# Paired 96-row loads, loads queued behind the moves, and no landing gate: a linear-attention and gated feed-forward kernel

## The chip, the cores and the metric

The kernel runs on one core of one Trainium2 chip. The metric is device time in microseconds (us); lower is better. The core has five engines that run side by side and wait for each other by semaphores: PE (matrix multiply), DVE (vector), ACT (scalar activation), POOL (GpSimd) and SP (SyncE, which here only issues DMA transfers). Each engine works through its own instructions in order, so an instruction that waits holds up everything behind it on that engine.

## The reference

A recurrent attention (a decaying state for each head) feeds a gated feed-forward block with a three-tap convolution. Cut to what matters:

```python
# batch 4, heads 8, sequence 768, head size 48; d_ff 1024
for t in range(S):
    cur = einsum('bhd,bhe->bhde', u * k[t], v[t])
    y[t] = einsum('bhd,bhde->bhe', r[t], state + cur)
    state = w * state + einsum('bhd,bhe->bhde', k[t], v[t])
x = y.transpose(0, 2, 1, 3).reshape(B, S, 384)
h = maximum(x @ w_in, 0)                        # 384 -> 1024
conv_out = sum over k of conv_w[k] * h shifted by k - 1
out = (h * sigmoid(conv_out)) @ w_out           # 1024 -> 384
```

## The kernel before

**Tiling.** The sequence is cut into 24 groups of 128 tokens (6 to a batch), each of two chunks of 64. The 8 heads are 4 pairs; in each pair x=0 is the even head and x=1 the odd one. For a group the core loads `KR` (k and r with the head dimension on partitions: even heads on rows 0 to 47, odd heads on rows 64 to 111, 4 KB to a row), and `TOK` (k, r and v with tokens on partitions). In HBM a group's `krd` block has 112 rows: odd heads in rows 0 to 47, 16 filler rows, even heads in rows 64 to 111. There are four buffers of each tile (NBUF). A group is brought in by five transfers in `load(g)`: two of 48 rows for `KR` (192 KB each), one of 128 rows for k and r of `TOK` (384 KB), two of 64 rows for v (96 KB each).

**Stages.** `prep(g)` multiplies `KR` by powers of the decay (DVE, one instruction of 112x1024, called KR below) and works on `TOK` (three products, mostly on POOL, a reduction QQ on DVE, and the diagonal SC). `visit(g, av, su)` is one run of small matmuls on PE: for group g the outputs AV, and for group g+1 the scores SP and the state update UP. Visit numbers below count from 1: visit 1 holds only the scores and update of group 0; visit n holds the outputs of group n-2 and the scores of group n-1. Behind it ACT (XH) and DVE (XL) split the outputs into two parts in `XT`, and six DMA moves of 16 rows each (L628) put the fourth head pair's rows in place. For the first NSEL=3 groups PE does this itself, by an extra pass over that pair (`av3`, copies `Y7`, selection matmuls `SEL`), and there are no moves.

`first(i)` (f1) is a tile of the first feed-forward product: 9 matmuls into one of three PSUM buffers HP, then on ACT a rectifier, one tap (CV) and a sigmoid (SG), on DVE two more taps (L656) and the gate (L660), then the gated tile split for `second` (f2), the second product. There are 8 units of some 384 tokens with 8 f1 tiles each; unit 0 needs the outputs of groups 0 to 2, unit 1 those of groups 2 to 5. The weights come in 8 pieces of w_in and 6 of w_out (`convert`: ACT, DVE TENSOR_SCALAR and SCALAR_TENSOR_TENSOR, then a cast and a remainder) through three staging buffers ST.

**What sets the order.** All instructions are first recorded with estimated durations; `Plan.order` simulates the engines with these numbers and puts out one fixed order for each engine. A transfer is entered with its share x of transfer time, scaled by XFER. `gate(i)` is the landing gate: a load or weight transfer (class ld or wd) may not start before the transfers sent ahead of it, but for the last AHEAD=2.5 of x, have landed; L746 turns this into a real wait on the chip. The moves (class mv) are not gated. Where PE has nothing to do for a while the plan lets it run small fill matmuls (L740) with no use for the result.

Apart from the gate, the transfers use eight completion counters in turn (DMAHW0 to 7 in the rows below), and a transfer waits for the one that had its counter before it, eight transfers earlier.

```python
for x in (1, 0):        # L385, in load(g)
    dma([], [...], KR[i][64 * x:64 * x + D], krd[g, 64 - 64 * x:112 - 64 * x], 0.45, 0.63, "ldK")
...
PE.matmul(UP[rows[x], n:n + D], TOK[j][xs[x], 0, p, c], TOK[j][xs[x], 2, p, c], start=True, stop=True)   # L572
...
visit(g, True, g + 1 < NG)      # L711
if g + NBUF < NG:
    load(g + NBUF)              # L713: no read named, so the plan is free to put it ahead of the moves
```

## Time and profile before

| | us |
|---|---|
| three runs | 311.65, 308.57, 311.37 |
| their median | 311.37 |
| the profiled execution, from outside | 310.83 |
| its span, first to last instruction | 309.1 |
| its mean granted PE clock | 0.989 of full speed |

The profile is one execution. Its times are counted from the start of the span; 310.83 - 309.1 = 1.73 us lie around it. "Busy" of PE counts its fill matmuls too. A row of the timeline gives start, length, engine, line, operation, tiles and count, and in brackets the idle time of the engine ahead of it and what ended that. A transfer's row on SP is its issue; it lands some microseconds later. In the waits view the row "SPq ... <- DMA" is time in which the issuing queue stood still until some transfer had landed.

### The profile page before, as it was taken

Reading aid. Unit: us, or ns where it says so; the run is one execution under the profiler, and the core shown is the slowest. Engines: PE = TensorE matmul, PEld = TensorE weight load, DVE = VectorE, ACT = ScalarE, POOL = GpSimd, SP = SyncE. Lnnn points to the kernel's source line nnn. Section 1 sums busy time; section 2 is a strip of 40 time slices with the busy share of each in tenths; the row PEclk is TensorE's granted clock in tenths of the full one; section 3 lists DMA queues with packets and bytes.
Section 4 is the critical chain, followed back from the end, with each engine's and each line's share of the span. In section 5 each row is a group of like instructions: output and inputs, shape, how many; then the busy total and the mean of one; then the engine's idle time right before and its main releaser. Section 6 shows DMA issues by size and latency. Waiting matters only on the chain.

```text
span 309.1 us, 10281 instructions
## 1 busy us (share of the span) xinstructions
PE 282.5 (91%) x4272; PEld 262.0 (85%) x4272; DVE 222.8 (72%) x400; ACT 178.0 (58%) x395; POOL 170.8 (55%) x202
## 2 busy tenths in 40 slices
...
GB/s 178 214 212 216 222 225 130 182 184 210 204 156 104 213 179 130 120 119 90 123 76 154 94 114 131 160 104 106 125 56 38 30 14 39 38 27 27 0 51 51
DMA packets 24654, 37.46 MB, mean 121 GB/s; under 512 B 4832, under 2 KB 18208, under 8 KB 24608
## 3 DMA queue, kind: packets, MB, share of 16 engines
...
q8 instruction: 33, 0.54, 0.8%
q10 hardware_dynamic: 304, 0.59, 0.6%
q14 instruction: 13, 0.11, 0.1%
HBM read 30.01 MB, written 4.72 MB: 112 GB/s over the span
## 4 chain that ended last, share of the span: by engine, by line
PE 51%; DMA 20%; DVE 11%; POOL 6%; ACT 6%; issue 3%; SPq 2%; DVEq 0%; ACTq 0%; POOLq 0%
PE HP L647 19%; PE PO L680 19%; DMA TOK<-in_krt_dram 7%; DMA KR<-in_krd_dram 6%; DVE CV L656 4%; PE SP L562 4%; PE HP L680 3%; DMA ST<-in_w_in_dram 3%; PE AV L575 2%; POOL TOK L358 2%; POOL GG L358 2%; PE AV L568 2%; DMA XT<-XT 2%; PE UP L572 2%; DVE SG L660 2%
## 5 line engine op out<-in xcount | busy, mean ns | idle before, releaser
L647 PE MATMUL HP<-XT,wi 128*128 128x384 f32 (+1 forms) x576 | 115.0, 344 | 13.0 <-DVE SG L660 5.3
L647 PEld LDWEIGHTS HP<-XT,wi 128*128 128x128 f32 x576 | 103.0, 191 | 16.6 <-DVE SG L660 6.6
L680 PE MATMUL PO<-GG,wo 128*128 128x382 f32 (+1 forms) x528 | 106.1, 343 | 2.9 <-issue 1.4
L680 PEld LDWEIGHTS PO<-GG,wo 128*128 128x128 f32 x528 | 92.0, 189 | 6.2 <-ACT OS L686 2.7
L358 POOL TENSOR_TENSOR GG<-SG,GG 128x386 fp32r<-128x386 f32 (+1 forms) x46 | 46.8, 1018 | 82.8 <-ACT GG L662 82.8
L656 DVE SCALAR_TENSOR_TENSOR CV<-HP,cw,CV 128x382 f32<-128x382 f32 (+1 forms) x128 | 78.0, 614 | 19.3 <-ACT CV L653 17.8
L659 ACT ACTIVATE SG<-CV 128x382 f32<-128x382 f32 (+1 forms) x64 | 33.5, 524 | 44.2 <-DVE CV L656 43.6
L660 DVE TENSOR_TENSOR SG<-HP,SG 128x382 f32<-128x382 f32 (+1 forms) x64 | 35.5, 554 | 20.8 <-ACT SG L659 20.5
L575 PE MATMUL AV<-SC,TOK 64*48 64x64 f32 x768 | 46.4, 218 | 0.8 <-DVE SC L589 0.8
L562 PE MATMUL SP<-KR 48*64 48x64 f32 x768 | 46.0, 230 | 0.1
L568 PE MATMUL AV<-KR,SS 48*48 48x64 f32 x704 | 43.2, 219 | 3.1 <-DVE XT L358 3.1
L662 ACT CAST GG<-SG 128x382 fp32r<-128x382 f32 (+1 forms) x64 | 32.7, 511 | 20.4 <-DVE SG L660 19.8
L562 PEld LDWEIGHTS SP<-KR 48*64 48x64 f32 x768 | 38.1, 134 | 6.2 <-issue 4.2
L572 PE MATMUL UP<-TOK 64*48 64x48 f32 x704 | 40.5, 206 | 0.4 <-DVE SS L358 0.4
L652 ACT ACTIVATE HP<-HP 128x384 f32<-128x384 f32 (+1 forms) x64 | 30.4, 476 | 15.6 <-PE HP L647 15.3
L358 DVE TENSOR_TENSOR KR<-KR,TKR 112x1024 f32<-112x1024 f32 (+1 forms) x26 | 29.3, 1132 | 12.8 <-DMA KR<-in_krd_dram 12.5
L653 ACT ACTIVATE CV<-HP,cw 128x382 f32<-128x382 f32 (+1 forms) x64 | 37.1, 580 | 1.0
L575 PEld LDWEIGHTS AV<-SC,TOK 64*48 64x48 f32 x768 | 35.2, 120 | 1.1 <-DVE SC L589 1.1
L568 PEld LDWEIGHTS AV<-KR,SS 48*48 48x48 f32 x704 | 32.0, 120 | 4.1 <-DVE XT L358 3.8
L572 PEld LDWEIGHTS UP<-TOK 64*48 64x48 f32 x704 | 33.0, 123 | 0.6 <-DVE SS L358 0.6
L358 POOL TENSOR_TENSOR TOK<-TOK,TH 128x384 f32<-128x384 f32 x24 | 24.7, 1028 | 10.5 <-DVE TOK L358 9.4
L508 POOL TENSOR_TENSOR SC<-eye,QQ 128x512 f32<-128x512 f32 x23 | 24.1, 1046 | 6.9 <-PE AV L575 3.1
...
## 6 DMA issues: line engine op xcount, KB each, us to landing
...
XT<-XT SPq DMA_DIRECT2D x126, 16.0 KB, 1.9
```

The source lines that it names most:

```text
L358: op(eng, d, rd, wr, lambda e: e.tensor_tensor(**kw), cls, port=not psum)
L562: PE.matmul(SP_[xs[x], p, c], KK[j][rows[x], p, t], RR[j][rows[x], p, t], start=True, stop=True)
L568: PE.matmul(outs[x], state(2 * g + c)[rows[x], p], RR[i][rows[x], p, t], start=not sel, stop=False)
L572: PE.matmul(UP[rows[x], n:n + D], TOK[j][xs[x], 0, p, c], TOK[j][xs[x], 2, p, c], start=True, stop=True)
L575: PE.matmul(outs[x], TOK[i][xs[x], 2, p, c], SC[g % 2][xs[x], p, c], start=first and c == 0 and not sel, stop=True)
L647: PE.matmul(hp, wi[a][:, j, fs], X[:, x, j, t], start=(j == 0 and k == 0), stop=(j == 2 and k == 2))
L653: op("act", act(n, 0.155), [H_, "cw"], [("T", ti)], lambda e: A.activation(t1, hp[:, 1:n + 1], AF.Copy, scale=cw[:, 3 * f + 1:3 * f + 2]), ...
L656: op("dve", dve(n) + 0.06, [H_, "cw"], [("T", ti)], lambda e, k=k: V.scalar_tensor_tensor(out=t1, in0=hp[:, k:n + k], scalar=cw[:, 3 * f + ...
L659: op("act", act(n, 0.097), [("T", ti)], [("SG", ti)], lambda e: A.activation(sg, t1, AF.Sigmoid))
L660: op("dve", dve(n), [H_], [("SG", ti)], lambda e: V.tensor_tensor(out=sg, in0=hp[:, 1:n + 1], in1=sg, op=ALU.mult), "GG")
L662: op("act", act(n), [("SG", ti)], [("GH", gi)], lambda e: A.copy(gh, sg))
L680: PE.matmul(po[:, :n], wo[a][:, f, ms], g2[x], start=(f == 0 and j == 0), stop=(f == NF - 1 and j == 2))
```

## The change

- **One transfer for two groups' halves.** Rows 64 to 111 of group g's block (even heads) and rows 0 to 47 of the next one's (odd heads) lie next to each other in HBM. `load_kr(g)` brings these 96 rows in one transfer into rows 16 to 111 of the `KR` tile (g+1) mod 4. A tile thus holds the even heads of g and the odd heads of g+1. A transfer of 48 rows (odd heads of group 0) goes ahead of them, and the last one has 48 rows. So 25 `KR` transfers stand in place of 48, and 25 decay products in place of 24; the first two tiles are done in halves. The load sent after visit g's part is `load_kr(g+3)`, where `KR` of g+4 went before; `TOK` stays at g+4.
- **Rows 0 to 15** of `KR` are zero (Z=16). The x=0 matmuls contract 64 rows instead of 48, and the x=0 weights of UP have 64 columns instead of 48 (`TOK` has 16 more words ahead of its data).
- **Loads behind the moves.** `moved(g)` makes a load "read" the last move of group g, so the plan puts it behind that move on SP.
- **No landing gate.** AHEAD=100 is never reached, so L746's waits go. The eight completion counters stay.
- **NSEL=2.** Group 2 loses its selection pass and gets six moves.
- Estimates: XFER 1.3 to 1.1, and other x for nearly every transfer. A clearing of UP goes, four of 128x16 in `TOK` come, the `KR` clearings have other rows.

```diff
-NSEL = 3
-AHEAD = 2.5
+NSEL = 2
+AHEAD = 100.0
+XK = 1.1
+HR = slice(0, 64), slice(64, 112)
+DR = slice(Z, 64), slice(64, 112)
-SWITCH, XFER = 0.13, 1.3
+SWITCH, XFER = 0.13, 1.1
...
+        rows_ = krd.rearrange("g q a p t -> (g q) a p t")
+        def moved(g):
+            return [("Xm", g // GPB % 2, g % GPB, 64, 2)] if g >= NSEL and AFTER else []
+        def load_kr(g, rd=()):
+            i = (g + 1) % NKR
+            a, b = 112 * g + 64, 112 * g + 64 + 2 * D
+            lo, hi = DR[0].start, DR[1].stop
...
+            dma(rd, ks, KR[i][lo:hi], rows_[a:b], 0.45, XK, "ldK")
-        def load(g, eng="sp"):
+        def load(g, eng="sp", rd=()):
             i = g % NBUF
-            for x in (1, 0):
-                dma([], [(n, i, x) for n in ("KK", "RR")], KR[i][64 * x:64 * x + D], krd[g, 64 - 64 * x:112 - 64 * x], 0.45, 0.63, "ldK")
-            dma([], [("tK", i), ("tR", i)], TOK[i][:, 0:2], krt[g], 0.55, 1.05, "ldT", eng)
+            dma(rd, [("tK", i), ("tR", i)], TOK[i][:, 0:2], krt[g], 0.55, 0.98, "ldT", eng)
...
-        op("dve", 0.7, [], ["SUu"], lambda e: V.memset(UP, 0.0))
...
-                        rows = [slice(64 * x, 64 * x + D) for x in range(2)]
+                        rows = HR
-                                PE.matmul(SP_[xs[x], p, c], KK[j][rows[x], p, t], RR[j][rows[x], p, t], start=True, stop=True)
+                                PE.matmul(SP_[xs[x], p, c], KK[tj[x]][rows[x], p, t], RR[tj[x]][rows[x], p, t], start=True, stop=True)
-                                PE.matmul(UP[rows[x], n:n + D], TOK[j][xs[x], 0, p, c], TOK[j][xs[x], 2, p, c], start=True, stop=True)
+                                PE.matmul(UP[rows[x], n:n + D], TOKP[j][xs[x], Z * x + (2 * p + c) * D:Z + (2 * p + c + 1) * D], TOK[j][xs[x], 2, p, c], start=True, stop=True)
...
+                if g + NKR - 1 < NG:
+                    load_kr(g + NKR - 1, moved(g))
                 if g + NBUF < NG:
-                    load(g + NBUF)
+                    load(g + NBUF, rd=moved(g))
```

The first place is SP where the tiles are loaded for the second time. ST is a staging buffer of weights, the number behind a tile's name is its buffer, the last number can be passed over; a wait DMAHWn is one for a transfer to land. Before (from the fifth group's k and r on):

```order
L362 DMA TOK0_65<-in_krt_dram 128x768 [waits DMAHW7_49,DVE_49,PE_49]
L362 DMA KR0_61<-in_krd_dram 48x1024 [waits DMAHW4_49,DMAHW1_49,PE_49]
L362 DMA KR0_61<-in_krd_dram 48x1024 [waits DMAHW2_49]
L362 DMA TOK0_65<-in_vt_dram 64x384 [waits DMAHW6_49,PE_49]
L362 DMA TOK0_65<-in_vt_dram 64x384 [waits DMAHW3_49,PE_49]
L362 DMA TOK1_66<-in_krt_dram 128x768 [waits DMAHW0_49,DVE_49,PE_49]
L362 DMA KR1_62<-in_krd_dram 48x1024 [waits DMAHW4_49,PE_49]
L362 DMA KR1_62<-in_krd_dram 48x1024 [waits DMAHW5_49]
L362 DMA ST0_103<-in_w_in_dram 128x768 [waits DMAHW7_49,DVE_49,Pool_49]
```

And now, from the same transfer up to the first move:

```order
L369 DMA TOK0_65<-in_krt_dram 128x768 [waits DVE_49,DMAHW6_49,PE_49,Pool_49]
L369 DMA ST2_105<-in_w_in_dram 128x768 [waits DMAHW7_49]
L369 DMA KR0_61<-in_krd_dram 96x1024 [waits DMAHW0_49,PE_49]
L369 DMA TOK0_65<-in_vt_dram 64x384 [waits DMAHW1_49,PE_49]
L369 DMA TOK0_65<-in_vt_dram 64x384 [waits DMAHW2_49,PE_49]
L369 DMA TOK1_66<-in_krt_dram 128x768 [waits DMAHW3_49,DVE_49,PE_49]
L369 DMA ST0_103<-in_w_in_dram 128x768 [waits DMAHW4_49,Pool_49]
L369 DMA KR1_62<-in_krd_dram 96x1024 [waits DMAHW5_49,PE_49]
L369 DMA TOK1_66<-in_vt_dram 64x384 [waits DMAHW6_49,PE_49]
L369 DMA TOK1_66<-in_vt_dram 64x384 [waits DMAHW7_49,PE_49]
L369 DMA ST1_104<-in_w_in_dram 128x768 [waits DMAHW0_49,Pool_49]
L369 DMA XT0_79<-XT0_79 16x2x128 [waits DMAHW1_49,DVE_49]
```

The counters now simply come round in turn (6, 7, 0, 1 ...), where before other landings stood among them; the fifth weight piece (the reload of ST1, which waits for POOL) stands ahead of group 2's moves.

The second place is DVE ahead of the first f1 tile's taps, the first row on a CV tile. PO is the buffer of a weight piece in conversion, and one TENSOR_SCALAR and one SCALAR_TENSOR_TENSOR on ST make up one piece. Before:

```order
L589 COPY_PREDICATED SC1_70<-mask_110,SP_120 128x512
L358 TENSOR_TENSOR XT0_79<-AV_122,XT0_79 128x3x128
L358 TENSOR_TENSOR SS0_71<-MM1_76,UP_121 112x192
L358 TENSOR_TENSOR KR1_62<-KR1_62,TKR_123 112x1024
L528 TENSOR_REDUCE QQ0_77<-TOK0_65 128x8
L475 TENSOR_SCALAR PO_127<-PO_127 128x384
L477 SCALAR_TENSOR_TENSOR ST0_103<-ST0_103,PO_127 128x384
L656 SCALAR_TENSOR_TENSOR CV0_83<-HP0_124,cw_119,CV0_83 128x382 x2
```

And now:

```order
L507 SCALAR_TENSOR_TENSOR ST1_104<-ST1_104,PO_127 128x384
L365 TENSOR_TENSOR wi1_116<-ST1_104,wi0_115 128x3x128
L562 TENSOR_REDUCE QQ1_78<-TOK1_66 128x8
L365 TENSOR_TENSOR SS1_72<-MM0_75,UP_121 112x192
L624 COPY_PREDICATED SC0_69<-mask_110,SP_120 128x512
L365 TENSOR_TENSOR XT0_79<-AV_122,XT0_79 112x4x128
L365 TENSOR_TENSOR SS2_73<-MM1_76,UP_121 112x192
L505 TENSOR_SCALAR PO_127<-PO_127 128x384
L507 SCALAR_TENSOR_TENSOR ST2_105<-ST2_105,PO_127 128x384
L691 SCALAR_TENSOR_TENSOR CV0_83<-HP0_124,cw_119,CV0_83 128x382
```

Before, the piece shown is the fourth; now it is the sixth, and visit 5 and the split of group 3's outputs also stand ahead of the first tap. On PE, visit 5 and 18 fill matmuls ahead of it now come before the first f1 tile, where before visit 4 was followed by 8 fills and two f1 tiles. From visit 8 on PE's order of visits, f1 and f2 is the same as before.

More of the change, by code (lines that the diff above doesn't have):

```diff
@@ L28 @@
 NBUF = 4
+NKR = 4
+AFTER = 1
+Z = 16
 NT = 3
@@ L310, in sb @@
             return [cst.tile(shape, dt, name=f"{name}{i}") for i in range(n)]
-        KR = sb([112, 2, NP, GT], F32, "KR", NBUF)
+        KR = sb([112, 2, NP, GT], F32, "KR", NKR)
         KK, RR = [x[:, 0] for x in KR], [x[:, 1] for x in KR]
-        TOK = sb([128, 3, NP, 2, D], F32, "TOK", NBUF)
+        TOKP = sb([128, Z + 3 * NP * 2 * D], F32, "TOK", NBUF)
+        TOK = [x[:, Z:].rearrange("q (a p c d) -> q a p c d", a=3, p=NP, c=2) for x in TOKP]
         SC = sb([128, NP, 2, C], F32, "SC", 2)
@@ L378, in krz @@
         def krz(i):
-            op("pool" if i else "dve", 1.0, [], [n for n in kr(i) if n[2] == 0], lambda e: e.memset(KR[i][32:64], 0.0), "KRz")
+            n = 64 if i == 0 else Z
+            op("pool" if i > 1 else "dve", 1.0, [], [n for n in kr(i) if n[2] == 0], lambda e: e.memset(KR[i][0:n], 0.0), "KRz")
         krz(0)
-        def load(g, eng="sp"):
+        krz(1)
+        for i in range(NBUF):
+            op("pool", 0.06, [], [("tK", i)], lambda e, i=i: G.memset(TOKP[i][:, 0:Z], 0.0), "KRz")
@@ new lines, in rwkv_ffn_kernel @@
+        rows_ = krd.rearrange("g q a p t -> (g q) a p t")
[5 more added lines that the diff above has]
+            lo, hi = DR[0].start, DR[1].stop
+            if g < 0:
+                a, lo = 0, 64
+                b = D
+            if g == NG - 1:
+                b, hi = a + D, 64
+            ks = [k for k in kr(i) if (k[2] == 0 or hi > 64) and (k[2] == 1 or lo < 64)]
+            dma(rd, ks, KR[i][lo:hi], rows_[a:b], 0.45, XK, "ldK")
@@ L392, in rwkv_ffn_kernel @@
+        load_kr(-1)
+        load_kr(0)
         load(0, "act")
-        dma([], ["uu"], uu, ut, 0.55, 0.4, "ldU")
+        dma([], ["uu"], uu, ut, 0.55, 0.25, "ldU")
         op("pool", 0.1, [], ["mask"], lambda e: G.memset(mask, 1))
         op("pool", 0.1, [], ["ident"], lambda e: G.memset(ident, 1.0))
+        for o, n, b in ((0, 64, Z), (64, 48, 0)):
+            op("pool", 0.2, [], ["ident"], lambda e, o=o, n=n, b=b: G.affine_select(
+                out=ident[o:o + n], in_=ident[o:o + n], pattern=[[1, D]],
+                compare_op=ALU.is_equal, fill=0.0, base=b, channel_multiplier=-1))
@@ L407, in rwkv_ffn_kernel @@
                 compare_op=ALU.is_equal, fill=0.0, base=0, channel_multiplier=-1))
-        for i in range(1, NBUF):
+        for i in range(2, NKR):
             krz(i)
```

39 lines of the change are left out of this document (21 added, 18 removed).

## The prediction, made before the changed kernel was run

> **What bounds the kernel now.** I read the page's busy line first, then PE's rows with idle time ahead of them, then the chain of work that ended last, then SP's queue.
>
> The page's first part, then PE's busy time by stage (columns: stage, its length, busy time of PE, weight loads, DVE, ACT, POOL, PE's granted clock, share and rate of the DMA engines):
>
> ```profile
> PE 282.5 (91%) x4272; PEld 262.0 (85%) x4272; DVE 222.8 (72%) x400; ACT 178.0 (58%) x395; POOL 170.8 (55%) x202
> ```
> ```profile
> 34.14:66.72 32.58, 26.24 (x463) 22.93 (x463) 28.06 (x53) 24.42 (x57) 27.44 (x29) 0.95 0.64 184
> 66.72:136.87 70.15, 64.40 (x1019) 60.25 (x1019) 57.90 (x100) 44.17 (x97) 55.17 (x59) 1.00 0.60 161
> 136.87:309.10 172.23, 165.17 (x2192) 159.54 (x2192) 112.81 (x200) 98.06 (x209) 62.04 (x69) 1.00 0.27 76
> ```
>
> The stages are cut where units begin: the first f1 tile starts at 34.14, unit 1's at 66.72. PE is the bound from 136.87 on (7.1 us idle in 172). Ahead of that it is fed too slowly: 6.3 us idle in the second stage, where DVE is busy 86%, and 5.8 in the third. PE's large gaps:
>
> ```profile
> 34.14 2.10 PE L647 MATMUL HP<-XT,wi 128*128 128x384 f32 x8 [1.47 <-ACT XT L618]
> 57.08 3.28 PE L647 MATMUL HP<-XT,wi 128*128 128x384 f32 x10 [2.52 <-DVE SG L660]
> 66.72 1.85 PE L647 MATMUL HP<-XT,wi 128*128 128x388 f32 x9 [0.85 <-DMA XT<-XT]
> 87.34 1.87 PE L647 MATMUL HP<-XT,wi 128*128 128x388 f32 x9 [0.78 <-DVE SG L660]
> 136.87 1.46 PE L647 MATMUL HP<-XT,wi 128*128 128x388 f32 x6 [2.17 <-DVE QQ L528]
> 171.21 1.82 PE L647 MATMUL HP<-XT,wi 128*128 128x384 f32 x9 [2.17 <-DMA XT<-XT]
> ```
>
> The chain shows why the feed is slow: loads one behind another, each sent only when an earlier one has landed.
>
> ```profile
> 23.05 5.60 DMA TOK<-in_krt_dram
> ...
> 29.29 5.71 DMA TOK<-in_krt_dram
> ...
> 35.06 4.07 DMA ST<-in_w_in_dram
> ...
> 39.19 5.36 DMA TOK<-in_krt_dram
> ...
> 44.61 1.02 POOL TOK L358
> ```
>
> The buffer of the load at 39.19 came free with visit 4 (28.71 to 31.6, below). It is sent 7.6 us later, behind the landings above, and POOL starts on it at 44.61. SP's waits say the same: on k and r of TOK alone the queue stood 24.8 us for landings.
>
> ```profile
> SPq L362 <- DMA TOK<-in_krt_dram: 24.8, 15, 3.6
> ```
>
> **The change part by part.** *Transfer.* At 143.91 both 48-row halves of KR run alone, then at 151.69 the 128 rows of TOK, with KR behind them (SP's issues, then the DMA rate, the last column):
>
> ```profile
> 143.91 0.79 SPq L362 DMA_DIRECT2D KR<-in_krd_dram  x2
> ...
> 151.69 0.53 SPq L362 DMA_DIRECT2D TOK<-in_krt_dram  x1
> 152.35 0.81 SPq L362 DMA_DIRECT2D KR<-in_krd_dram  x2
> ```
> ```profile
> 144.75:145.50 0.75, 0.75 (x6) 0.75 (x5) 0.75 (x2) 0.73 (x4) 0.75 (x1) 1.00 0.81 202
> 153.50:154.75 1.25, 1.25 (x8) 1.25 (x8) 1.25 (x3) 0.53 (x1) 0.73 (x2) 1.00 1.00 357
> 154.75:155.75 1.00, 1.00 (x7) 1.00 (x7) 0.88 (x3) 0.08 (x1) 0.51 (x1) 1.00 0.97 223
> ```
>
> So 48 rows move at 202 to 223 GB/s with the engines nearly full, 128 rows at 357. The pair's 393 KB take 1.76 to 1.95 us; at TOK's rate 1.10. The 96 rows are nearer to 128 than to 48, so I take 0.7 us less of DMA time a group (0 to 0.85). It counts only where a landing ends a wait, that is through the terms below; one issue fewer saves SP some 0.4 us (0.79/2).
>
> The Trainium skill, "SBUF — State Buffer", section "Door 1: The DMA port swizzle", says that rows 0 to 63 reach only eight of SBUF's sixteen DMA ports and rows 64 to 127 the other eight. By its 218 and 436 GB/s the pair would take an estimated 1.80 us and the joint transfer 0.90, so 0.9 saved where my rows give 0.7. The trace agrees in kind, 202 to 223 against 357, and the measured rates decide.
>
> *Start of the first f1 tile.* Group 2 trades its selection pass for six moves. The rows that price it:
>
> ```profile
> 26.25 0.32 PE L568 MATMUL AV<-KR,SS 48*48 48x64 f32 x4 [2.13 <-DVE XT L358]
> 28.71 0.37 PE L562 MATMUL SP<-KR 48*64 48x64 f32 x2
> 31.62 1.05 PE L740 MATMUL HP<-wz 128*128 128x256 bf16 x8
> ```
> ```profile
> L624 ACT CAST XT<-AV 112x512 fp32r<-112x512 f32 x21 | 12.3, 586 | 4.1 <-PE AV L575 3.1 <-PE UP L572 1.0
> L358 DVE TENSOR_TENSOR XT<-AV,XT 112x512 fp32r<-112x512 f32 x21 | 14.2, 679 | 0.0
> L362 SPq DMA_DIRECT2D XT<-XT x126: 585/592/1632, 45.9 to 264.8; - x126
> DMA to landing us min/median/max: 1.8/1.9/6.3
> ```
> ```profile
> 30.20 1.03 POOL L358 TENSOR_TENSOR wi<-ST,wi 128x384 fp32r<-128x384 f32 x1
> 8.65 1.28 DVE L358 TENSOR_TENSOR KR<-KR,TKR 112x512 f32<-112x512 f32 x2 [0.31 <-ACT TKR L440]
> ```
>
> Without av3 and its copies visit 4 can stand where av3 stood, 26.25 (it waited for the split of group 1). It lasts 2.9 us (28.71 to 31.62), so 29.15; XH 0.59 and XL 0.68: 30.4; six issues at 0.592: 34.0; landing 1.9: 35.9. Late bound: the moves stand on SP behind the fifth weight piece, whose buffer POOL gives free when the second piece's remainder is done, 31.2 in the row: 31.2 + 3.55 + 1.9 = 36.7. The extra product of the first tile (half products of two tiles, 1.28 us more on DVE ahead of visit 1) could push all that to 38.0. I take 36.5: later than before's 34.14 by 2.4, but with visit 5 already done.
>
> *Unit 0, 34.14 to 66.72.* DVE works 28.06 us of 32.58.
>
> ```profile
> L475 DVE TENSOR_SCALAR PO<-PO 128x384 int32<-128x384 int32 (+2 forms) x11 | 6.1, 552 | 2.7 <-ACT PO L472 2.7
> L477 DVE SCALAR_TENSOR_TENSOR ST<-ST,PO 128x384 int32<-128x384 int32 (+1 forms) x10 | 5.7, 575 | 0.1
> L589 DVE COPY_PREDICATED SC<-mask,SP 128x512 f32<-128x512 int32 x24 | 17.7, 739 | 0.6 <-PE UP L572 0.5
> L358 DVE TENSOR_TENSOR SS<-MM,UP 112x192 f32<-112x192 f32 x40 | 13.7, 343 | 0.9 <-POOL MM L605 0.9
> ```
> ```profile
> 36.25 1.22 DVE L358 TENSOR_TENSOR KR<-KR,TKR 112x1024 f32<-112x1024 f32 x1 [1.31 <-DMA KR<-in_krd_dram]
> 55.87 0.70 DVE L475 TENSOR_SCALAR PO<-PO 128x512 int32<-128x512 int32 x1 [1.25 <-ACT PO L472]
> ```
>
> Two to three more weight pieces are now converted ahead of f1 (2.5 x 1.13 = 2.8 us), and visit 5's mask and two state sums (0.74 + 0.69 = 1.4). Left: 28.06 - 2.8 - 1.4 = 23.9. Of the 4.5 us idle, 1.31 and 1.25 follow from late landings (ACT's PO waits for a weight load); I let half of these go, so 3.2 stay. Unit 1 then begins at 36.5 + 23.9 + 3.2 = 63.6, 3.1 us earlier than 66.72. Bounds: 38.0 + 23.9 + 4.5 = 66.4 (0.3 gained), and 35.9 with all landing waits gone (2.0 idle): 61.8, 4.9 earlier.
>
> *Units 1 and 2.* The gaps at 87.34 and 136.87 are DVE standing in order at a KR product whose load has not landed:
>
> ```profile
> 85.59 1.22 DVE L358 TENSOR_TENSOR KR<-KR,TKR 112x1024 f32<-112x1024 f32 x1 [2.39 <-DMA KR<-in_krd_dram]
> ```
>
> I take half of 0.78 + 2.17, so 1.5 (0 to 2.95). *Later.* At 171.21 the unit waits for its last moves. Six issues and a landing stay, TOK and v still stand ahead, only KR's two issues leave: 0.4 of 2.17 (0 to 0.8). On the other side 176 weight loads of UP get 64 columns instead of 48. Weight loads of 48 and 64 columns take 123 and 134 ns here:
>
> ```profile
> L572 PEld LDWEIGHTS UP<-TOK 64*48 64x48 f32 x704 | 33.0, 123 | 0.6 <-DVE SS L358 0.6
> L562 PEld LDWEIGHTS SP<-KR 48*64 48x64 f32 x768 | 38.1, 134 | 6.2 <-issue 4.2 <-DVE CV L656 0.5 <-DVE SC L589 0.4
> ```
>
> With two records each, 352 x 11 ns = 3.9 us if all showed, 0 if matmuls cover them. The x=1 load of 48 columns runs beside, so I take 0.5. Contracting 64 rows instead of 48 changes no count of columns; I price it at 0 inside that bound. Clearings and the lost clearing of UP lie before DVE's first product at 8.65, where the decay powers set the time: 0.
>
> *Sum.* 309.1 - 3.1 - 1.5 - 0.4 + 0.5 = 304.6 for the span; with the 1.73 around it 306.3 for such an execution. The median of the runs is 0.54 above the profiled one (311.37 against 310.83), so **306.9**.
>
> **Rivals.** *A, more goes:* f1 at 35.9, all waits for landings gone: 309.1 - 4.9 - 2.95 - 0.8 + 2.27 = 302.7 (2.27 = 1.73 + 0.54). For it: the chain above is nearly all landings. Against: DVE and POOL are busy over 78% up to 136.87.
>
> *B, hidden or not done:* the gate goes, but every transfer still waits for the one eight places earlier, and KR's lead is a visit shorter. f1 at 38.0, DVE's waits unchanged: unit 1 at 66.4, nothing gained later, 0.5 lost on UP: 309.1 - 0.3 + 0.5 + 2.27 = 311.6. For it: SP also waits for ACT and PE, which the change leaves. Against: the 7.6 us at 39.19.
>
> *C, slower by moves behind loads.* Up to eight transfers may be under way and the gate no longer keeps the queue short, so a unit's last moves land late, PE waiting as at 66.72 and 171.21. Landings reach 6.3 us in the row above, where 1.9 is the median. If the seven later units each start 1.5 us later: 306.9 + 10.5 = 317.4. From 0.64 us a unit (4.5/7) the gain is used up. Against it: the loads are now put behind the moves of the same group.
>
> The Trainium skill bears on C: "DMA: Bandwidth & Descriptors", section "Queues, rings and completion order", has each DMA engine take its descriptors in the order of the ring, so that a move would queue behind every load sent before it.
>
> **How the numbers follow.** Forecast 0.50, A 0.16, B 0.22, C 0.12. A measurement of this kernel tells about 1% (3.1 us) from no change, so faster is below 308.3, slower above 314.5. Faster: A and nearly all of the forecast's cases, 0.62; same: B and the forecast's rest, 0.27; slower: C's larger part, 0.11. The range 301.5 to 313 takes in A and B and leaves out C and a little of A.
>
> **What would show it.** Right: the first f1 later, near 36.5, with visit 5 ahead of it; unit 1's first tile near 63.6; KR's DMA rate near 350 GB/s; SP's wait for TOK landings well under 24.8; no KR wait over 2 us on DVE near 136. Wrong: unit 1 no earlier than 66, moves landing in over 3 us at unit starts (C), or visits longer by 0.1 us and more (UP's weights).

## The result, and the profile after

The changed kernel takes 311.93 us (median of 20 runs, 309.13 to 313.48), the kernel before 310.16 us in the same series (20 runs, 304.64 to 315.16). The ratio of after to before is 1.013, with a 95% interval of 1.0085 to 1.0174: a little slower, where 306.9 us and faster was forecast, and inside the band that the prediction called no change (308.3 to 314.5). Each ratio in this document leaves out a kernel's runs over 1.5% above its fastest (here 14 of the 20 of before, none of after), so it makes after look slower than the two medians over all runs do, which lie 0.6% apart (1.8 us). The profiled execution of after has a span of 311.7 us (313.4 from outside), that of before 309.1.

The page's first part for after, and PE's busy time by stage, cut where it was for before and with the stretch ahead (the columns are the same):

```profile
PE 283.1 (91%) x4249; PEld 264.1 (85%) x4249; DVE 229.0 (73%) x411; ACT 177.1 (57%) x401; POOL 160.4 (51%) x194
```
```profile
10.43:34.14 23.71, 18.19 (x532) 15.57 (x532) 14.02 (x27) 9.59 (x29) 21.42 (x24) 0.93 0.85 237
34.14:66.72 32.58, 23.88 (x443) 21.52 (x444) 26.18 (x50) 22.12 (x54) 21.50 (x24) 0.90 0.55 161
66.72:136.87 70.15, 67.04 (x1038) 63.44 (x1037) 61.10 (x106) 46.48 (x107) 49.50 (x53) 1.00 0.51 148
136.87:311.70 174.83, 165.97 (x2191) 159.45 (x2189) 119.89 (x212) 95.95 (x207) 61.83 (x68) 1.00 0.27 82
```

PE is busy as long as before (283.1 us against 282.5). Between 34.14 and 66.72 it is idle 8.7 us, where it was 6.3, and DVE, which had the most to do there, is less busy than before (26.2 against 28.1), so it waits more. The DMA engines are busier ahead of that (237 GB/s from 10.43 to 34.14, before 216) and less busy in it (161 against 184). In the next stretch PE is idle 3.1 us instead of 5.8, a gain; in the last 8.9 instead of 7.1. PE's rows with idle time, and the starts of unit 0 (40.17) and unit 1 (69.11):

```profile
35.92 0.27 PE L597 MATMUL SP<-KR 64*64 64x64 f32 x2 [2.25 <-DVE SC L624]
40.17 2.00 PE L682 MATMUL HP<-XT,wi 128*128 128x384 f32 x10 [0.30 <-DMA XT<-XT]
48.03 0.27 PE L597 MATMUL SP<-KR 64*64 64x64 f32 x2 [2.87 <-DVE KR L365]
58.22 0.33 PE L597 MATMUL SP<-KR 64*64 64x64 f32 x4 [2.00 <-DVE KR L365]
69.11 1.84 PE L682 MATMUL HP<-XT,wi 128*128 128x388 f32 x9
```

The large gaps of before (57.08, 136.87, 171.21) are gone. New ones stand ahead of visits 6 and 7, both for DVE's product on KR.

PE's granted clock also halves here in three stretches of 3.4 us (from 12.2, 36.1 and 60.0; in before in two, from 26.7 and 57.4), and the matmuls in them take longer: the three of f1 in the last stretch take 522 to 686 ns, where the median of all is 338 (the clock is the third column from the end; the second row gives ns, least, median and most):

```profile
60.01:63.42 3.41, 3.08 (x77) 2.88 (x68) 3.41 (x8) 3.37 (x8) 3.17 (x4) 0.50 0.11 24
```
```profile
L682 PE MATMUL HP<-XT,wi x576: 331/338/686, 40.2 to 293.6; 128*128 128x384 f32 x96, 128*128 128x388 f32 x96
```

Each stretch begins within 2 us of a gap of PE (ahead of 12.06, 35.92 and 58.22), but the longest gap, ahead of 48.03, has none behind it. What sets the clock no run tests.

The waits of all engines (what waited, for what: total us, times, longest):

```profile
POOL TOK L365 <- DMA TOK<-in_krt_dram: 25.7, 13, 3.7
DVE KR L365 <- DMA KR<-in_krd_dram: 15.1, 15, 2.6
PE PO L715 <- ACT OS L721: 6.9, 9, 1.2
```
```profile
SPq L369 <- DMA TOK<-in_krt_dram: 8.0, 6, 3.5
```

SP waits 8.0 us for TOK landings where it waited 24.8. But DVE now waits for KR 15 times, 15.1 us in all (before: 8 times, 12.5 us), and PE waits at PO for the output copy OS nine times (before: twice, 1.4 us). POOL's wait for TOK grows most, from 4.5 us; but it is still 15.5 us in e10 below, the fastest of all runs. The waits for KR and at PO belong together, as one place late in the span shows (start, length, engine, line, operation; in brackets the idle time ahead and what ended it):

```profile
188.74 1.22 DVE L365 TENSOR_TENSOR KR<-KR,TKR 112x1024 f32<-112x1024 f32 x1 [1.52 <-DMA KR<-in_krd_dram]
...
191.37 0.60 DVE L691 SCALAR_TENSOR_TENSOR CV<-HP,cw,CV 128x382 f32<-128x382 f32 x1
192.05 0.52 ACT L694 ACTIVATE SG<-CV 128x382 f32<-128x382 f32 x1 [4.69 <-DVE CV L691]
...
192.89 0.47 ACT L721 ACTIVATE OS<-PO 128x386 f32<-128x386 f32 x1
...
193.42 1.32 PE L715 MATMUL PO<-GG,wo 128*128 128x386 f32 x6 [1.21 <-ACT OS L721]
```

DVE stands 1.52 us at a product whose load has not landed. The taps CV stand behind that on DVE, the sigmoid SG waits for them on ACT, the copy OS, which frees PO, stands behind SG on ACT, and PE waits for PO. Read from the bottom the row names ACT; the one that is late is a DMA several steps away.

Why it is late: SP's issues of moves and KR loads, and DVE's products:

```profile
35.00 4.86 SPq L369 DMA_DIRECT2D XT<-XT  x6
...
41.05 0.38 SPq L369 DMA_DIRECT2D KR<-in_krd_dram  x1
...
43.84 5.07 SPq L369 DMA_DIRECT2D XT<-XT  x5
...
50.28 0.58 SPq L369 DMA_DIRECT2D XT<-XT  x1
50.96 0.52 SPq L369 DMA_DIRECT2D KR<-in_krd_dram  x1
```
```profile
46.76 1.22 DVE L365 TENSOR_TENSOR KR<-KR,TKR 112x1024 f32<-112x1024 f32 x1 [1.18 <-DMA KR<-in_krd_dram]
...
56.94 1.22 DVE L365 TENSOR_TENSOR KR<-KR,TKR 112x1024 f32<-112x1024 f32 x1 [2.62 <-DMA KR<-in_krd_dram]
```

The load behind the product of 46.76, which visit 6 needs, is sent at 41.05; in the kernel before the one for visit 6 went out at 29.91. A joint tile holds the even heads of one group and the odd heads of the next, so it serves one visit more than a tile of one group did. With four buffers its successor can go out one visit later. It also stands behind the moves now (those of group 2 end their issue at 39.86, those of group 3 at 50.86). Which of the two counts, and what the lost gate does, the trace alone can't say.

### The profile page after: what moved, and what is told of

Read it like the earlier page. It is cut to its first block, busy times and chain, and to the rows that moved or that the text cites. A ratio compares the mean times of both kernels' runs of the same rounds, so it can differ in the third digit from the quotient of the medians.

```text
span 311.7 us, 10202 instructions
## 1 busy us (share of the span) xinstructions
PE 283.1 (91%) x4249; PEld 264.1 (85%) x4249; DVE 229.0 (73%) x411; ACT 177.1 (57%) x401; POOL 160.4 (51%) x194
## 4 chain that ended last, share of the span: by engine, by line
PE 33%; DMA 21%; DVE 21%; POOL 8%; ACT 7%; SPq 5%; issue 4%; ACTq 0%; POOLq 0%
PE PO L715 15%; DMA KR<-in_krd_dram 13%; PE HP L682 12%; DMA TOK<-in_krt_dram 6%; DVE CV L691 6%; SPq L369 5%; POOL TOK L365 5%; DVE KR L365 4%; PE HP L715 3%; DVE SG L695 3%; DMA ST<-in_w_in_dram 2%; ACT SG L694 2%; DVE SC L624 2%; DVE XT L365 2%; DVE GG L365 2%
## 5 line engine op out<-in xcount | busy, mean ns | idle before, releaser
L682 PE MATMUL HP<-XT,wi 128*128 128x384 f32 (+1 forms) x576 | 112.8, 341 | 2.5 <-DVE SG L695 2.1
L365 POOL TENSOR_TENSOR GG<-SG,GG 128x382 fp32r<-128x382 f32 (+1 forms) x37 | 37.6, 1017 | 70.4 <-ACT GG L697 70.2
L597 PE MATMUL SP<-KR 48*64 48x64 f32 (+1 forms) x768 | 50.1, 237 | 9.4 <-DVE KR L365 6.1
L597 PEld LDWEIGHTS SP<-KR 48*64 48x64 f32 (+1 forms) x768 | 44.4, 141 | 15.3 <-DVE KR L365 5.5
L607 PE MATMUL UP<-TOK 64*48 64x48 f32 (+1 forms) x704 | 45.7, 217 | 1.5 <-POOL TOK L365 1.2
L603 PE MATMUL AV<-KR,SS 64*48 64x64 f32 x704 | 44.6, 223 | 2.4 <-DVE XT L365 2.2
L607 PEld LDWEIGHTS UP<-TOK 64*48 64x48 f32 (+1 forms) x704 | 41.7, 136 | 2.0 <-POOL TOK L365 1.3
L365 DVE TENSOR_TENSOR KR<-KR,TKR 112x1024 f32<-112x1024 f32 (+1 forms) x27 | 30.6, 1139 | 15.5 <-DMA KR<-in_krd_dram 15.1
L610 PEld LDWEIGHTS AV<-SC,TOK 64*48 64x48 f32 x768 | 38.2, 124 | 0.2 <-DVE SC L624 0.2
L603 PEld LDWEIGHTS AV<-KR,SS 64*48 64x48 f32 x704 | 34.6, 124 | 3.2 <-DVE XT L365 2.9
L365 POOL TENSOR_TENSOR TOK<-TOK 128x384 f32<-128x384 f32 x23 | 23.3, 1011 | 25.8 <-DMA TOK<-in_krt_dram 25.7
```

The lines of the kernel that those rows point to most:

```text
L365: op(eng, d, rd, wr, lambda e: e.tensor_tensor(**kw), cls, port=not psum)
L597: PE.matmul(SP_[xs[x], p, c], KK[tj[x]][rows[x], p, t], RR[tj[x]][rows[x], p, t], start=True, stop=True)
L603: PE.matmul(outs[x], state(2 * g + c)[rows[x], p], RR[ti[x]][rows[x], p, t], start=not sel, stop=False)
L607: PE.matmul(UP[rows[x], n:n + D], TOKP[j][xs[x], Z * x + (2 * p + c) * D:Z + (2 * p + c + 1) * D], TOK[j][xs[x], 2, p, c], start=True, sto ...
L610: PE.matmul(outs[x], TOK[i][xs[x], 2, p, c], SC[g % 2][xs[x], p, c], start=first and c == 0 and not sel, stop=True)
L682: PE.matmul(hp, wi[a][:, j, fs], X[:, x, j, t], start=(j == 0 and k == 0), stop=(j == 2 and k == 2))
```

## The experiments

Times are medians; "against before" is the difference to the median of the kernel before in the same series (310.2 to 312.3 us). Where it and the ratio point apart (e2, e15), neither is read as a change against before. KR is DVE's wait for KR loads, PO is PE's wait at PO for OS, clock is PE's mean granted clock, all three of the profiled execution (before: 12.5, 1.4, 0.989). For e7 and e13 that execution took 321.6 and 315.9 us, more than their medians, for e8 305.9 us, 5 us less than its median.

The plan makes a new order for each edit, so no run changes one thing alone: with the gate off (e6), for example, ACT has 411 instructions where it had 395. And the runs made from the kernel before keep the old estimates (XFER and x), those made from the changed kernel have the new ones; no run changes the estimates by themselves.

| run | us | against before | ratio (95%) | KR | PO | clock |
|---|---|---|---|---|---|---|
| the changed kernel | 311.9 | +1.8 | 1.013 (1.009 to 1.017) | 15.1 | 6.9 | 0.984 |
| e1_before_wide | 310.4 | -1.6 | 1.000 (0.995 to 1.005) | 11.5 | 1.4 | 0.989 |
| e2_no_tie | 310.9 | -1.1 | 1.008 (1.003 to 1.013) | 12.0 | 3.8 | 0.988 |
| e3_three_sel | 315.9 | +3.9 | 1.011 (1.005 to 1.018) | 10.7 | 3.0 | 0.978 |
| e4_gate | 317.6 | +5.6 | 1.021 (1.016 to 1.026) | 16.0 | 7.0 | 0.973 |
| e5_before_short_lead | 319.1 | +6.8 | 1.028 (1.022 to 1.035) | 22.6 | 6.0 | 0.973 |
| e6_before_no_gate | 305.7 | -6.6 | 0.988 (0.980 to 0.996) | 1.1 | 0.3 | 0.977 |
| e7_fewer_gg | 320.1 | +7.8 | 1.027 (1.018 to 1.036) | 27.1 | 5.5 | 0.973 |
| e8_five_kr | 311.3 | -1.1 | none given | 10.4 | 5.0 | 1.000 |
| e9_no_gate_short_lead | 308.0 | -2.8 | 0.988 (0.983 to 0.992) | 10.7 | 5.8 | 0.983 |
| e10_five_kr_whole | 302.1 | -8.7 | 0.968 (0.964 to 0.973) | 2.7 | 1.3 | 0.993 |
| e11_pair_only | 308.6 | -2.2 | 0.991 (0.987 to 0.994) | 2.5 | 1.4 | 0.978 |
| e12_no_gate_tied | 309.7 | -1.1 | 1.001 (0.996 to 1.005) | 8.3 | 6.1 | 0.983 |
| e13_all_but_pair | 313.3 | +2.3 | 1.012 (1.008 to 1.016) | 10.1 | 7.4 | 0.967 |
| e14_five_untied | 307.1 | -3.9 | 0.991 (0.987 to 0.996) | none | none | 0.976 |
| e15_five_three_sel | 310.0 | -1.0 | 1.004 (1.000 to 1.008) | 7.4 | 4.6 | 0.983 |
| e16_five_gate | 315.4 | +4.4 | 1.021 (1.015 to 1.027) | 12.8 | 4.2 | 0.976 |
| e17_halves_untied_two | 319.1 | +8.1 | 1.032 (1.023 to 1.042) | 7.6 | 10.9 | 0.957 |

### The wider matmuls alone

e1 is the kernel before with this:

```diff
-rows = [slice(64 * x, 64 * x + D) for x in range(2)]
+rows = [slice(0, 64), slice(64, 112)]
-PE.matmul(UP[rows[x], n:n + D], TOK[j][xs[x], 0, p, c], ...)
+PE.matmul(UP[rows[x], n:n + D], <64 columns from there on for x=0, 48 for x=1>, ...)
```

> The kernel before, with one part of the change alone: the even heads' small matmuls contract 64 rows instead of 48 and the weights of UP for the even heads have 64 columns instead of 48 (the 16 extra columns meet cleared rows or are not read). Theory 1 (the wider small matmuls are paid on PE where it bounds): the later units, 32.1 us long without their gaps in the kernel before, become 32.3 to 32.5, weight loads of UP go from 123 to about 136 ns, and the time is about 2.3 us above the kernel before (ratio 1.007). Rival (they run beside other work, and the longer units of the changed kernel have another cause): weight loads grow but the units stay at 32.0 to 32.1, ratio 1.000 to 1.002.

The rival holds. The weight loads of UP grow (count, busy us, mean ns; 123 ns in the kernel before), the three units from 170.51 on are 31.9 to 32.0 us long, and the ratio is 1.0001 (0.995 to 1.0051).

```profile
L573 PEld LDWEIGHTS UP<-TOK 64*48 64x48 f32 (+1 forms) x704 | 38.4, 129 | 0.6 <-DVE SS L358 0.6
```

### The changed kernel with one part undone

e2: `AFTER = 1` to `0`. e3: `NSEL = 2` to `3`. e4: `AHEAD = 100.0` to `2.5`.

> The changed kernel, with its loads no longer put behind the moves of the group (AFTER = 0); all else stays. Theory 1 (loads stand behind the moves on SP with a lead one visit shorter, so KR lands late for DVE's product): the wait of DVE's KR products falls from 15.1 us to under 8, PE's gaps of 2.87 and 2.00 us at 48.03 and 58.22 go or halve, unit 1 begins near 66 instead of 69.1 and the time is 2 to 4 us below the changed kernel, near the kernel before (ratio to before 1.000 to 1.006). Rival (the tie protects the moves): KR lands earlier, but a unit's last moves land over 3 us after their issue and f1 waits for them by about 1.5 us a unit, time 3 to 8 us above the changed kernel (ratio 1.02 to 1.04).

> The changed kernel, with group 2's selection matmuls back in place of its six moves (NSEL = 3); all else stays. Theory 2 (six moves for group 2 delay the first f1 and with it all of unit 0): the first f1 tile starts near 35 instead of 40.17, unit 1 near 66 instead of 69.1, time 2 to 3 us below the changed kernel (ratio to before 1.003 to 1.007). Theory 1 (the late KR loads set unit 0's end): the first f1 starts earlier, but the KR waits near 48 and 58 stay and unit 1 begins at 68 to 69, time within 1 us of the changed kernel (ratio 1.010 to 1.016).

> The changed kernel, with the gate back: each load again waits until few others are on their way (AHEAD = 2.5); all else stays. Theory 3 (many loads under way at once share the DMA engines and the early ones land late, TOK of group 1 after 9.3 us): TOK of group 1 lands near 10 instead of 13.1, POOL's wait for TOK falls from 25.7 us to under 12, the first f1 starts 1 to 3 us earlier and the time falls by 1 to 3 us (ratio to before 1.003 to 1.010). Theory 1 (what is late is the load behind the moves, whatever is under way): SP's waits for TOK landings come back (over 15 us instead of 8.0), KR's waits stay or grow, and the time is equal or up to 3 us above the changed kernel (ratio 1.012 to 1.022).

e2 bears out neither theory in full. KR falls only to 12.0, not under 8. Visit 6 starts at 43.32 instead of 48.03, but PE waits 3.37 us for moves at unit 1, which begins at 69.69; the time is 1.0 us lower, and the intervals of the two ratios overlap. So the place behind the moves alone is not the cause. e3 lets theory 2 fall: the first f1 still starts at 38.69, not near 35, and the time does not fall (the ratio, 1.011, is in theory 1's range; unit 1 begins at 67.05, earlier than that theory had it). e4 speaks against theory 3: with the gate back the time is no lower (ratio 1.021, as theory 1 had it), POOL's wait for TOK is 19.4 us, not under 12, and KR stays at 16.0. With any one of the three undone the kernel is no faster than 310.9 us: none of them alone is what ate the gain. All three still have the short lead.

### Lead and gate on the kernel before

e5 gives KR its own count of buffers, three instead of four; e6 takes off the gate; e9 does both.

```diff
+NKR = 3
-KR = sb([112, 2, NP, GT], F32, "KR", NBUF)
+KR = sb([112, 2, NP, GT], F32, "KR", NKR)
...
+    if g + NKR < NG:
+        load_kr(g + NKR)
     if g + NBUF < NG:
         load(g + NBUF)
```
```diff
-AHEAD = 2.5
+AHEAD = 100.0
```

> The kernel before with three buffers for KR instead of four, so that each KR load can be sent one visit later, as in the changed kernel; transfers, gate and all else stay. Theory 4 (the joint tile serves one visit more, so its load goes out one visit later, and that is what makes the start of the changed kernel late): DVE's wait for KR loads grows from 12.5 us to over 16, unit 1 begins at 68 to 70 instead of 66.7, time 2 to 4 us above the kernel before (ratio 1.006 to 1.013). Rival (the lead is long enough; it is the place behind the moves or the lost gate): unit 1 within 0.7 us of 66.7, ratio 0.997 to 1.003.

> The kernel before with the gate alone taken off (AHEAD = 100): no load waits for others to land; halves, lead, order rules and selection passes stay. Forecast's theory (the gate held the feed back): SP's wait for TOK landings falls from 24.8 us to under 10, loads of visits 5 and 6 land 1 to 3 us earlier, unit 1 begins 1 to 2 us earlier, time 1 to 3 us below the kernel before (ratio 0.990 to 0.997). Rival (the gate kept the queue short for those that are needed first): early landings share the DMA engines and moves land later, time equal to or up to 4 us above (ratio 1.000 to 1.013).

> The kernel before with two parts of the change and no others: the gate off (AHEAD = 100) and three KR buffers, so that each KR load goes out one visit later as in the changed kernel; halves, UP, selection passes and the place of the loads stay. Theory 4 (gate and lead together are the whole of what the change does to the time; the first is worth -6.6 us of medians by itself, the second +6.8): time 309 to 314 us, within 2 us of the changed kernel, unit 1 at 67 to 69, DVE's KR waits 10 to 18 us. Rival (without the gate the loads are early enough with the short lead too, and the joint transfer, the tie or the moves cost the changed kernel its time): 304 to 308 us as with the gate off alone.

e5, then e6, the waits:

```profile
DVE KR L359 <- DMA KR<-in_krd_dram: 22.6, 11, 3.5
...
PE PO L687 <- ACT OS L693: 6.0, 8, 2.1
```
```profile
DVE KR L358 <- DMA KR<-in_krd_dram: 1.1, 1, 1.1
...
PE PO L680 <- ACT OS L686: 0.3, 1, 0.3
```

One visit less of lead costs the kernel before 6.8 us, more than the 2 to 4 expected, and brings the pattern of after: late KR, then PO. Taking off the gate by itself gains 6.6 us (1.2% by the ratio, 0.4 to 2.0), and both waits all but vanish. That is about the whole forecast (4.5 us), from one constant. e9, with both, takes 308.0 us, in the rival's range, although its KR waits (10.7) and its unit 1 (67.06) are as theory 4 had them; by the ratios it is as fast as e6 (0.988 both). So without the gate the short lead costs these halves nothing that is clear, and gate and lead are not the whole of the change: between e9 and the changed kernel some 4 to 5 us (2.5% by the ratios) are left for its other parts.

e6 also shows where the gain lies. PE's stretches, cut where unit 1 begins (68.60):

```profile
0.00:68.60 68.60, 56.91 (x1080) 45.80 (x1080) 54.42 (x106) 36.40 (x90) 53.65 (x75) 0.90 0.80 206
68.60:136.87 68.27, 66.88 (x1042) 64.52 (x1042) 58.39 (x102) 48.29 (x112) 50.32 (x54) 1.00 0.61 158
136.87:302.40 165.53, 160.93 (x2171) 155.74 (x2169) 113.70 (x204) 96.35 (x209) 56.40 (x62) 1.00 0.26 76
```

Unit 1 begins 1.9 us later than in the kernel before (66.72). From there to the end it takes 302.4 - 68.6 = 233.8 us, where before takes 309.1 - 66.7 = 242.4 and after 311.7 - 69.1 = 242.6. PE is idle 1.4 us between 68.6 and 136.87.

### A fifth KR buffer

It needs 4 KB a partition more, room that the changed kernel does not have. e8 took it from GG, with e7 as control; e10 instead lets small tiles share room with tiles that are used at other times, which adds one small copy. No run shares the room without the fifth buffer. With it the plan also gives DVE, ACT, POOL and SP another order than in after; that of PE is nearly the same.

```diff
-NGB = 13
+NGB = 11                                   # e7, e8
```
```diff
-NKR = 4
+NKR = 5                                    # e8, e10
-PW = sb([112, NP, 96], F32, "PW")          # from here: e10
+PW = CV[1][0:112, 0:NP * 96].rearrange("q (p n) -> q p n", p=NP)
-SEL, Y7 = sb([112, 3, 64], F32, "SEL"), sb([112, GT], F32, "Y7")
+SEL = OS[0][0:112, 0:192].rearrange("q (p n) -> q p n", p=3)
+Y7 = OS[0][0:112, 192:192 + GT]
...
```

> The changed kernel with eleven buffers for GG instead of thirteen: the control for the next run, which needs the room. Both theories expect the same: the changed kernel's time or up to 2 us above it (ratio to before 1.005 to 1.018), KR waits of 14 to 17 us on DVE as in the changed kernel.

> The changed kernel with five KR buffers (and eleven for GG, as the control), so that the lead of the KR loads is that of the kernel before again; loads still stand behind the moves. Theory 4 (the lead): DVE's KR waits fall from 15 us to under 8, the gaps of 2 to 3 us ahead of visits 6 and 7 go, unit 1 begins 2 to 3 us earlier than in the control, time 2 to 4 us below it (ratio to before 0.997 to 1.006). Rival (the place behind the moves, or DMA load as such): KR waits stay above 12 us and the time is within 1 us of the control.

> The changed kernel with a fifth KR buffer and thirteen GG buffers (small tiles that are used at other times share room to make place), so the joint transfer goes out as early as the halves did before; loads still behind the moves. Theory 4 (the lead): DVE's KR waits fall from 15.1 us to under 9, unit 1 begins at 65 to 67, time 3 to 6 us below the changed kernel (306 to 309, ratio to before 0.980 to 0.995). Rival (the tie to the moves): KR waits stay above 12 us, time within 1.5 us of 311.9.

With eleven GG buffers, tiles of GG are written anew before the third block of columns of w_out has read them, so that part of the output is another; the work is the same. e7 misses its expectation (320.1 us): it is no control for the changed kernel, but it is one for e8, which is 8.8 us faster in the median with the fifth buffer (runs of 305.94 to 311.69 us against 316.70 to 324.67). e10 has none of this: 302.05 us, better than expected, the fastest of all runs, against before 0.968 (0.964 to 0.973). Its waits, DVE's products and SP's KR issues:

```profile
DVE KR L367 <- DMA KR<-in_krd_dram: 2.7, 4, 0.8
...
PE PO L718 <- ACT OS L724: 1.3, 3, 0.6
```
```profile
35.85 1.21 DVE L367 TENSOR_TENSOR KR<-KR,TKR 112x1024 f32<-112x1024 f32 x1
44.95 1.22 DVE L367 TENSOR_TENSOR KR<-KR,TKR 112x1024 f32<-112x1024 f32 x1 [0.50 <-DMA KR<-in_krd_dram]
```
```profile
26.88 0.33 SPq L371 DMA_DIRECT2D KR<-in_krd_dram  x1
39.27 0.38 SPq L371 DMA_DIRECT2D KR<-in_krd_dram  x1
```

The load of 39.27 goes out behind group 2's moves, nearly when its fellow of 41.05 did in after. But it serves visit 7 (product at 44.95), where the other served visit 6; visit 6 has the load of 26.88, and its product at 35.85 waits for nothing. Same queue, same place behind the moves, same transfer, one visit more of lead, and DVE's waits for KR fall from 15.1 to 2.7 us. Unit 1's first tile starts at 64.14:

```profile
64.14 1.84 PE L685 MATMUL HP<-XT,wi 128*128 128x388 f32 x9
```

That is 5.0 us earlier than in after; from there to the end it is 300.3 - 64.1 = 236.2 us instead of 242.6. The gain is in both.

### What the other parts are worth beside that

e12, e17 and e13 are the kernel before without the gate and, in this order, with loads tied (`rd` on the load transfers, as the change does it), with `NSEL = 2`, and with both. e14, e15, e11 and e16 are e10 with `AFTER = 0`, with `NSEL = 3`, with both, and with `AHEAD = 2.5`.

> As the run with the fifth KR buffer, and also the loads not put behind the moves (AFTER = 0) and group 2's selection matmuls back (NSEL = 3): what is left of the change is the gate taken off, the joint transfer and its matmuls. Theory 5 (the joint transfer saves DMA time, but no landing ends a wait any more once the gate is off): 304 to 308 us, as the kernel before with the gate off (305.7). Forecast's term (0.7 us of DMA time a group counts at the start): 300 to 304 us. Rival (the extra product and the half group fetched too early cost the start): 308 to 312 us.

> The kernel before with the gate off and the loads put behind the moves of the group whose visit frees their buffer; halves and the lead of four buffers stay. Theory 4 (what counts is the lead and the gate; the tie costs little): 305 to 308 us, within 2 us of the run with the gate off alone (305.7). Rival 1 (standing behind the moves is what makes loads late): 309 to 313 us, DVE's KR waits over 8 us. Rival 2 (the tie protects the moves): 302 to 305 us.

> The kernel before with the gate off, the loads behind the moves and two selection passes (NSEL = 2): the change without the joint transfer, its matmuls and its shorter lead. If the joint transfer is worth something by itself (0.7 us of DMA time a group, as the forecast has it), this is 2 to 5 us above the changed kernel with five KR buffers (304 to 307 against 302.1 us). If it is worth nothing (the lead was all), 301 to 303 us. If it costs (the extra product, wider matmuls, half a group fetched too early), 297 to 301 us.

> The changed kernel with five KR buffers and the loads not put behind the moves (AFTER = 0). If the tie protects the moves, unit starts wait for moves again (as 4.17 us at 71.48 in the run with the joint transfer only) and the time is 305 to 309 us; if it is the selection pass that costs there, 301 to 304 us.

> The changed kernel with five KR buffers and group 2's selection matmuls back (NSEL = 3), loads tied. If the selection pass costs (14 us of small matmuls and an ACT copy ahead of visit 2, as in the changed kernel, where putting it back made 311.9 into 315.9), 304 to 308 us; if it is the tie that matters, 301 to 304 us.

> The changed kernel with five KR buffers and the gate back (AHEAD = 2.5). If taking the gate off gains here as it does in the kernel before (6 us), 306 to 310 us; if the lead covers what the gate delays, 301 to 304 us.

> The kernel before with the gate off and two selection passes (NSEL = 2): halves, four KR buffers, loads not behind the moves. If the joint transfer gains by itself (forecast: 2 to 5 us), this is at 309 to 312 us against 307.07 of its partner with the joint transfer and five buffers. If it gains nothing outside the tied version, 304 to 308 us, near the run with the gate off alone (305.7).

Several miss: e12 is 4 us above e6 (rival 1: KR waits 8.3 us), e13 lies 11 us above e10 where 2 to 5 were expected, e15 2 us above its range, e16 5 us above, e17 7 us above. e11 lies just above theory 5's range, in the rival's; e14 is as the tie that protects the moves would have it. Eight of the runs make a table, all without the gate and with the same lead (ratios to before):

| | halves, four buffers | joint, five buffers |
|---|---|---|
| not tied, three passes | 0.988 (0.980 to 0.996), e6 | 0.991 (0.987 to 0.994), e11 |
| tied, three passes | 1.001 (0.996 to 1.005), e12 | 1.004 (1.000 to 1.008), e15 |
| not tied, two passes | 1.032 (1.023 to 1.042), e17 | 0.991 (0.987 to 0.996), e14 |
| tied, two passes | 1.012 (1.008 to 1.016), e13 | 0.968 (0.964 to 0.973), e10 |

By these ratios the joint transfer makes no clear difference in the first two rows and gains 4.1 and 4.4% in the last two (the columns differ in the estimates, too). The tie costs 1.3% with three passes and gains 2.0 and 2.3% with two. Two passes instead of three cost the halves 4.4 and 1.2%, change nothing in the untied joint version, and gain 3.6% in the tied one. So the parts hang together: undone one at a time in e10 (0.968), each costs something, the gate put back 5.3% (e16), the fifth buffer taken away 4.5% (the changed kernel), the halves 4.4% (e13, with the old estimates), the third pass 3.6% (e15), the tie left out 2.3% (e14).

The gate off gains 1.2% (before to e6), 4.1% (e5 to e9) and 5.3% (e16 to e10); from e4 to after it is 0.8%, with intervals that just overlap. One visit more of lead gains 2.8% (e5 to before), 4.5% (after to e10) and 1.7% (e2 to e14), and nothing clear in three other pairs (e9 to e6, e3 to e15, e4 to e16): in the changed kernel with the gate, or in the halves without it, these ratios show no gain. Neither part shows a clear loss anywhere.

Untied versions show what the tie is for. PE's wait for moves in e14 and the start of its unit 1, and SP ahead of it:

```profile
PE HP L685 <- DMA XT<-XT: 9.8, 2, 5.5
```
```profile
70.95 3.25 PE L685 MATMUL HP<-XT,wi 128*128 128x388 f32 x9 [5.46 <-DMA XT<-XT]
```
```profile
56.46 6.75 SPq L371 DMA_DIRECT2D XT<-XT  x6
63.31 0.53 SPq L371 DMA_DIRECT2D KR<-in_krd_dram  x1
63.94 0.52 SPq L371 DMA_DIRECT2D TOK<-in_vt_dram  x1
64.55 0.55 SPq L371 DMA_DIRECT2D ST<-in_w_out_dram  x1
65.19 3.77 SPq L371 DMA_DIRECT2D XT<-XT  x6
```

DVE waits for no KR load at all there. But the last moves of unit 1, whose split ends at 60.81, stand on SP behind six others that take 6.75 us and then behind three loads. They go out from 65.19 to 68.96, and f1 starts 2 us after that. Why the joint transfer gains only with two passes stays open: each edit also makes the plan put other rows in other places (in e13 TOK stands ahead of KR on SP, in e10 behind it), and no run separates that.

The granted clock is a rival for part of these differences. Over all runs it is 0.952 to 0.973 in e17, 0.971 to 0.983 in e6, 0.971 to 0.999 in after and 0.989 to 0.994 in e10. An estimate from these: mean time times the share of the clock that is missing is 12.5 us in e17, 6.7 in e6, 4.4 in after and 2.4 in e10. If PE had work throughout, the clock could make up 5.8 us of the 12.6 us between the means of e6 and e17, and 2.0 of the 10.0 between after and e10. No run holds it fixed.

## Why the prediction was wrong

The step that failed is the price of late KR loads. The prediction let half of unit 0's waits for late landings go ("I let half of these go, so 3.2 stay") and half of the gaps at 87.34 and 136.87. It had seen what works the other way, "KR's lead is a visit shorter", but only in rival B, and priced it there at no loss. DVE's waits for KR did not halve: they grew from 12.5 to 15.1 us. The sum in three steps (us of the profiled spans, 309.1 before and 311.7 after):

| | forecast | came |
|---|---|---|
| up to unit 1's start (66.72 before, 69.11 after) | -3.1 | +2.4 |
| from there to unit 4's start (171.21, 170.23) | -1.9 | -3.4 |
| from there to the end (0.5 was for UP in all visits) | +0.5 | +3.6 |

The first step fails at two of its terms. The first f1 starts at 40.17 instead of 36.5. And in unit 0 DVE is busy 24.09 us, as forecast (23.9), but idle 28.94 - 24.09 = 4.85 us where 3.2 were to stay; 3.80 of these are the two KR products at 46.76 and 56.94, shown above:

```profile
40.17:69.11 28.94, 22.67 (x331) 20.38 (x331) 24.09 (x45) 21.41 (x51) 18.91 (x19) 0.94 0.60 176
```

The second step went better than forecast, as the gaps at 87.34, 136.87 and 171.21 go. For the third the sum has no term: behind 170.23 PE waits for PO in four places, 3.45 us, as in the place shown at 193.42.

```profile
180.80 0.44 PE L715 MATMUL PO<-GG,wo 128*128 128x386 f32 x1 [0.82 <-ACT OS L721]
```
```profile
226.96 0.80 PE L715 MATMUL PO<-GG,wo 128*128 128x382 f32 x3 [1.18 <-ACT OS L721]
```

With the lead given back (e10) KR waits are 2.7 us and the time is 9.9 us lower (4.5% by the ratios); taken from the kernel before (e5) it costs 6.8 us. Rival B gave 311.6 us, and 311.9 came, but that is luck: B has unit 1 at 66.4, the short lead free and the gate's end hidden. The gate's end is worth 1.2% in e6 and 5.3% in e10; in the changed kernel, with its short lead, it is 0.8%, with intervals that just overlap (e4).

- *Transfer: right in rate.* A joint load that runs alone from 186.25 on (the issue, then DMA's share and rate in the last two columns):

```profile
184.00 1.35 SPq L369 DMA_DIRECT2D KR<-in_krd_dram  x1
```
```profile
186.25:186.50 0.25, 0.25 (x20) 0.25 (x16) 0.25 (x1) 0.25 (x1) 0.00 (x0) 1.00 0.50 164
186.50:187.00 0.50, 0.50 (x11) 0.42 (x6) 0.50 (x2) 0.29 (x2) 0.18 (x1) 1.00 1.00 385
```

  385 GB/s with the engines full, so 393 KB in 1.02 us; forecast 1.10, and 1.76 to 1.95 for the halves. The Trainium skill, "SBUF — State Buffer", section "Door 1: The DMA port swizzle", has partitions 0 to 63 and 64 to 127 on different ports, so that the joint transfer reaches both groups; by its 436 GB/s that would be an estimated 0.90 us. The trace agrees in kind, with 385 GB/s. From issue to landing it still takes 5.1 us in the median (a half took 4.6 in before), and that is what a lead must cover.
- *First f1 at 36.5 (35.9 to 38.0): too early.* It starts at 40.17, and at 38.39 in e10, which has the lead. Group 2's split on ACT was put at 29.15, the one on DVE right behind it, and six issues at 3.55 us. What came (after, timeline):

```profile
31.71 0.59 ACT L659 CAST XT<-AV 112x512 fp32r<-112x512 f32 x1 [0.62 <-PE AV L610]
...
33.15 1.22 DVE L365 TENSOR_TENSOR KR<-KR,TKR 112x1024 f32<-112x1024 f32 x1 [0.86 <-DMA KR<-in_krd_dram]
34.28 0.68 DVE L365 TENSOR_TENSOR XT<-AV,XT 112x512 fp32r<-112x512 f32 x1
```

  The split is 2.6 us later than that, because visit 4, put at 26.25, starts at 28.96; in e10 it starts at 28.48, so this part is not the lead's. Its DVE half then stands 2 us behind a KR product that waits for its load. The six issues take 4.86 us (35.00, above).
- *Unit 1 at 63.6: not reached.* 69.11. e10 has it at 64.14, still with a later f1 (38.39). As a sign of the gain unit 1 does not serve alone: e6 has it at 68.60, later than before, and gains 8.6 us behind it.
- *The 64-column weights (+0.5, 0 to 3.9): right.* 129 ns instead of 123, and no time that e1 can tell (its interval is some 1.6 us to either side).
- *Rival A* (all landing waits go, 302.7 us) is the time of the same change with one buffer more, 302.1, but not for A's reason: the first f1 is at 38.39, not 35.9, and POOL still waits 15.5 us for TOK.
- *Rival C* (late moves) is real where the tie is missing, at 3.4 to 5.5 us a place (e2, e11, e14), and absent in the changed kernel, whose moves land in 1.9 us. The Trainium skill's "DMA: Bandwidth & Descriptors", section "Queues, rings and completion order", has each DMA engine take descriptors in ring order, so that moves would queue behind loads. No run here singles that out; what these traces show is ahead of it: SP issues the moves late.
